# Attention: divisions of a pair in one step of 256 columns, and weight tiles scaled by ScalarE, signed by GpSimd and joined in two VectorE steps

## The chip, the core and the metric

One core of a Trainium2 chip runs the whole program. The metric is the device time of one execution in microseconds (us). TensorE (PE), VectorE (DVE), ScalarE (ACT) and GpSimd (POOL) each run their own instructions in order; SyncE (SP) and GpSimd's queue issue DMAs. An instruction that waits for another engine or for a DMA waits on a semaphore, and all that is queued behind it on its engine waits with it.

## The reference

All arrays are float32, except that the four large weight matrices (w_ch1, w_ch2, w_in, w_out) reach the kernel as float64: NumPy's division by a float64 root makes them so.

```
scores = q @ k.T / sqrt(64) + bias        # q, k, v: 4 batches, 8 heads, 576 rows, 64
scores = where(0 <= rel < 128, scores, -1e9)
attn   = exp(scores - max(scores))
attn   = attn / (sum(attn) + 1e-9)
x      = (attn @ v), heads joined         # 4 x 576 x 512
xn     = (x - mean) / sqrt(var + 1e-6) * g_ln
x      = x + relu(xn @ w_ch1) @ w_ch2     # 512 -> 2048 -> 512
h      = relu(x @ w_in)                   # 512 -> 1024
gate   = sigmoid(conv of 3 taps over the rows of h)
out    = (h * gate) @ w_out               # 1024 -> 512
```

## The kernel before

**Attention (L700 to L944).** Its 72 tiles (a tile is 128 query rows of two heads) go through a software pipeline that is written out by hand: 18 iterations, k = 0 to 17, of four tiles each, in two pairs a and b. In each, TensorE makes the scores of a pair in PSUM (`ps`, L737); VectorE joins two blocks (L748) and takes minima (L752); ScalarE makes the exponentials with their sums (L762, four of 128 columns in a pair); `shares` (L767) divides: VectorE adds 1e-9 and takes the reciprocal, and of a pair's four blocks of 128 columns the two of the even heads are multiplied by VectorE, those of the odd heads by GpSimd (L774). TensorE turns the shares (L784), ScalarE copies them (`pc`, L789), GpSimd masks them twice (`select_p`, L796), TensorE multiplies by v (L812), ScalarE writes the result into `x` (`outputs`, L825). TensorE also turns the q and k of the next tiles (`turn_qk`, L711), and ScalarE copies them (`qt`, `kt`, L838). One iteration's code holds work of three: scores of iteration k, shares of k-1, values of k-2 and outputs of k-3.

**Weights in the attention.** The chip has no float64, so a weight is made from its two 32-bit words, in four steps on a tile of 128 x 512: the high word is taken as a float and multiplied by 2^-112 (`rescale`, L350 on; on GpSimd L358, on ScalarE L356); VectorE shifts left by 3 and masks (part 0, L373), sets the sign bit from the high word (part 1, L378) and the lowest 3 bits from the low word (part 2, L383). Then ScalarE writes a rounded copy (high, L412), VectorE the rest (low, L415). Twelve tiles are converted in this way during the attention. `weights_step` does one step of a tile at a time, and `extras` (L841) calls it twice in an iteration: between `shares` of pair b of the iteration before and `values`, that is ahead of the new exponentials, and once at the end of the iteration. `FINE_START` and `FINE_AT` say in which of these half steps: the load, three half steps later the rescale, and then one step in each half step. So a rescale always falls ahead of the exponentials in the code, and a load at an iteration's end, on SP's queue, behind the loads of q, k and v for later tiles. These write into buffers that `turn_qk` must have read. The raw words of three tiles have room at a time.

**After the attention.** From L944 on the work is put in order by the class `Plan` (L36): each operation is given with its engine, a duration, the memory that it reads and writes, and for some an earliest time (`late`); `schedule` then picks, again and again, the operation that can start first, among those ready on an engine the one that is due first, with DMAs no further than 3 us ahead of a modelled bandwidth. The instructions are issued in that order. Twenty more weight tiles are converted here (`convert_next`, `convert` at L1047) from five raw slots: signs on GpSimd (`signs`, L364: the high word times 0.0, which leaves its sign), rescale on ScalarE, one VectorE step that shifts and joins the sign (L1064), part 2, the high copy, and the low part by a two-operand step of GpSimd (L1236). The matrix products of this stage are L1035.

Of the kernel before, what the change touches and what calls it, by code (L numbers as in the profile page):

```python
# [14 lines left out]
ALU = mybir.AluOpType  # L15
# [20 lines left out]
class Plan:  # L36
# [58 lines left out]
    def schedule(self, pe, goal, succ, cost, rate, landing, wait):  # L95
# [14 lines left out]
        free = {}  # L110
        lock = 0.0
        dma = 0.0
# [98 lines left out]
def tile_kernel(  # L211
# [183 lines left out]
    FINE = (("rescale",), (0,), (1,), (2,), ("high",), ("low",))  # L395

    def weights_step(stages, start=True, only=None):
# [3 lines left out]
        for j in range(max((len(do) for _, do in now), default=0)):  # L401
            for ld, do in now:
                if j >= len(do):
                    continue
                kind, i, raw = ld["kind"], ld["i"], ld["raw"]
                if do[j] == "rescale":
                    t = ld["t"] = fav(FA_CV0 + cvn[0] % 3 * 512, 512).bitcast(I32)
                    cvn[0] += 1
                    rescale(t, raw, G)
                elif do[j] == "high":  # L410
                    w = wtile(kind, i)
                    S.activation(w[:, 0, :], ld["t"].bitcast(F32), AF.Copy)  # L412
                elif do[j] == "low":
                    w = wtile(kind, i)
                    V.tensor_tensor(  # L415
                        out=w[:, 1, :], in0=ld["t"].bitcast(F32), in1=w[:, 0, :].bitcast(F32),
                        op=ALU.subtract,
                    )
                    flight.remove(ld)
                else:  # L420
                    to_f32(ld["t"], raw, (do[j],), ld["mid"])
        if todo and start:
# [9 lines left out]
            else:  # L432
# [3 lines left out]
                "kind": kind, "i": i, "pool": pool, "t": None, "mid": None, "only": only,  # L436
# [100 lines left out]
    with ExitStack() as actx:  # L537
# [229 lines left out]
        def shares(n: int):  # L767
# [5 lines left out]
            for i in range(4):  # L773
                (G if i % 2 else V).tensor_scalar(  # L774
                    out=pp[:, i, :], in0=pp[:, i, :], scalar1=sm[:, 1, i : i + 1], scalar2=1.0,
                    op0=ALU.mult, op1=ALU.mult,
                )
# [63 lines left out]
        def extras(n: int, m: int):  # L841
            for args in fine_at.get(n // 2 + m, ()):
                weights_step(FINE, *args)
# [201 lines left out]
    BF0 = 2000  # L1045

    def convert(kind: str, i: int, raw, cv, mid=None, eng="V"):  # L1047

        late_at = BF0 if raw is None else 0
        src = {"w1": w_ch1, "win": w_in, "w2": w_ch2, "wout": w_out}[kind]  # L1050
        if kind in ("w1", "win"):
            dma(
                raw.rearrange("p (c f) -> p c f", f=2 * P),
                src[:, 2 * i * P : 2 * (i + 1) * P].rearrange("(c p) f -> p c f", p=P), 524288,
            )
        else:
            dma(raw, src[i * P : (i + 1) * P, :], 524288)
# [165 lines left out]
    def convert_next():  # L1223
# [6 lines left out]
        convert(kind, f, raw, cv, MIDS[n % len(MIDS)])  # L1230
# [688 lines left out]
```

## Time and profile before

| | |
|---|---|
| time, median of 3 runs (lowest to highest) | 737.68 us (733.99 to 738.47) |
| the profiled execution, its span | 736.93 us, 735.2 us |
| TensorE busy | 712.5 us (97%) |
| VectorE busy | 526.2 us (72%) |
| ScalarE busy | 402.6 us (55%) |
| GpSimd busy | 238.3 us (32%) |
| the last chain of work | TensorE 71%, VectorE 12%, DMA 5%, GpSimd 5%, ScalarE 3% |

The shares of the whole span are means over stages: the attention ends near 147 us, and behind it come matrix products alone, with TensorE busy nearly throughout. So a stage's limit is read from the stage: from a table of the busy time in a stretch, and from the rows of an engine's timeline, where the number in brackets is the idle time just before an instruction and who ended it. Neighbouring instructions of an engine overlap at their ends, so what an instruction takes from its engine is read from two starts rather than from its duration.

### The profile page before, as it was taken

The numbers are of one execution on the slowest core, as the hardware profiler recorded it, in microseconds if no ns is written. First come the engines' busy times: TensorE is split into PE (matmuls) and PEld (weight loads), VectorE is DVE, ScalarE is ACT, GpSimd is POOL, SyncE is SP. The second block draws the span as 40 slices with busy tenths as digits, with TensorE's granted clock in tenths as the row PEclk, the third lists the DMA queues.
The fourth block names the chain that finished last, engine by engine and source line by source line (L and its number), as shares of the span: only waits on it lengthen the run. The fifth ranks groups of instructions, "written<-read, shape, count | busy, mean of one in ns | idle before, by whom it ended". The sixth has DMA issues, their size and how long they took to land.

```text
span 735.2 us, 13451 instructions
## 1 busy us (share of the span) xinstructions
PE 712.5 (97%) x4704; PEld 664.9 (90%) x4704; DVE 526.2 (72%) x1053; ACT 402.6 (55%) x1050; POOL 238.3 (32%) x408
## 2 busy tenths in 40 slices
PE   7999998899989999999999999999999999999998
PEld 6777876799989999999999999999999898998887
DVE  6799999567979726556679654568468998787731
ACT  4888877645424423333346333344377787776741
POOL 1778789759741202321220233242421000000000
PEclk9999999999999999999999999999999999999999
DMA  6777766238519926986860599996933000000011
GB/s 152 177 179 175 198 155 187 71 104 273 189 35 339 292 70 177 275 265 223 258 211 12 174 267 305 285 276 200 272 93 87 15 30 15 30 15 29 29 47 55
DMA packets 122303, 114.63 MB, mean 156 GB/s; under 512 B 63552, under 2 KB 87292, under 8 KB 122236
## 3 DMA queue, kind: packets, MB, share of 16 engines
q1 hardware_dynamic: 101020, 76.81, 34.6%
q0 software_dynamic: 20160, 36.71, 18.4%
q8 instruction: 37, 0.61, 0.3%
q10 hardware_dynamic: 1056, 0.26, 0.2%
q14 instruction: 30, 0.25, 0.1%
HBM read 80.70 MB, written 33.05 MB: 155 GB/s over the span
## 4 chain that ended last, share of the span: by engine, by line
PE 71%; DVE 12%; DMA 5%; POOL 5%; ACT 3%; issue 3%; SPq 0%; POOLq 0%; ACTq 0%; DVEq 0%
PE bank L1035 65%; DMA wind<-r 2%; PE ps L737 2%; DVE ps L748 2%; DVE pp L774 2%; DMA fa<-in_moe_w_in 1%; DVE mn L752 1%; POOL pt L796 1%; PE po L812 1%; DVE fa L383 1%; PE ptp L784 1%; POOL pp L774 1%; DVE fa L378 1%; ACT fa L996 1%; DMA xnb<-in_moe_w_ch 1%
## 5 line engine op out<-in xcount | busy, mean ns | idle before, releaser
L1035 PE MATMUL bank<-hhr,r 128*128 128x384 f32 x1152 | 214.0, 338 | 0.5 <-DVE fa L1003 0.5
L1035 PE MATMUL bank<-r,r 128*128 128x288 f32 (+1 forms) x1248 | 203.9, 314 | 1.3 <-ACT fa L996 1.1
L1035 PEld LDWEIGHTS bank<-hhr,r 128*128 128x128 f32 x1152 | 199.6, 188 | 2.5 <-DVE fa L1003 1.6
L1035 PEld LDWEIGHTS bank<-r,r 128*128 128x128 f32 x1248 | 193.9, 188 | 4.7 <-ACT fa L996 1.9
L1332 POOL DMA_DIRECT2D r<-w1d x96 | 51.9, 543 | 180.9 <-PE bank L1035 171.8
L996 ACT ACTIVATE fa<-bank 128x288 f32<-128x288 f32 (+1 forms) x112 | 49.8, 445 | 73.0 <-PE bank L1035 71.7
L1035 PE MATMUL bank<-r 128*128 128x512 f32 (+2 forms) x360 | 81.7, 372 | 0.1
L1035 PEld LDWEIGHTS bank<-r 128*128 128x128 f32 x360 | 63.6, 188 | 9.8 <-ACT r L1782 0.5
L996 ACT ACTIVATE r<-fa 128x256 fp32r<-128x256 f32 (+2 forms) x94 | 48.0, 521 | 39.0 <-DMA wind<-r 13.5
L996 ACT ACTIVATE hhr<-bank 128x384 fp32r<-128x384 f32 x46 | 22.5, 490 | 75.5 <-PE bank L1035 75.4
L1003 DVE TENSOR_TENSOR fa<-bank,fa 128x288 f32<-128x288 f32 (+1 forms) x88 | 43.6, 500 | 27.3 <-ACT fa L996 14.6
L762 ACT ACTIVATE pp<-ps,mn 128x128 f32<-128x128 f32 x144 | 51.4, 384 | 12.2 <-DVE mn L752 8.8
L774 POOL TENSOR_SCALAR pp<-pp,sm 128x128 f32<-128x128 f32 x72 | 43.6, 616 | 32.5 <-DVE sm L771 29.9
L1011 DVE SCALAR_TENSOR_TENSOR fa<-fa,cw 128x576 f32<-128x576 f32 x64 | 51.2, 813 | 1.5 <-ACT fa L996 0.7
L1003 DVE TENSOR_TENSOR r<-fa,r 128x256 fp32r<-128x256 f32 (+1 forms) x74 | 37.7, 521 | 19.3 <-ACT r L996 13.1
L1011 DVE SCALAR_TENSOR_TENSOR hhr<-bank,hhr 128x384 fp32r<-128x384 f32 x46 | 25.4, 552 | 35.2 <-ACT hhr L996 35.0
L796 POOL TENSOR_SCALAR_AFFINE_SELECT pt<-pc 128x512 f32<-128x512 f32 x72 | 46.7, 679 | 1.7 <-ACT pc L789 1.4
L737 PE MATMUL ps<-kt,qt 64*128 64x256 f32 x288 | 44.1, 400 | 2.6 <-ACT pp L762 1.7
L812 PE MATMUL po<-pt,rawv 128*64 128x128 f32 x544 | 37.9, 280 | 7.4 <-POOL pt L796 4.9
L1035 PE MATMUL bank<-r,hhr 128*128 128x512 f32 (+1 forms) x192 | 44.6, 381 | 0.0
L812 PEld LDWEIGHTS po<-pt,rawv 128*64 128x64 f32 x544 | 28.9, 136 | 16.0 <-POOL pt L796 12.6
L996 ACT ACTIVATE fa<-fa 128x576 f32<-128x576 f32 (+1 forms) x64 | 39.1, 620 | 2.7 <-DVE fa L1003 1.6
(146 smaller groups left out, 1138.0 us busy)
## 6 DMA issues: line engine op xcount, KB each, us to landing
r<-w1d POOLq DMA_DIRECT2D x96, 256.0 KB, 4.8
fa<-in_moe_w_ch SPq DMA_DIRECT2D x24, 512.0 KB, 4.8
w1d<-r SPq DMA_DIRECT2D x40, 256.0 KB, 3.5
wind<-r SPq DMA_DIRECT2D x28, 256.0 KB, 4.5
r<-wind POOLq DMA_DIRECT2D x28, 256.0 KB, 4.8
out<-h SPq DMA_DIRECT2D x17, 256.0 KB, 2.0
rawq<-in_q SPq DMA_DIRECT2D x32, 128.0 KB, 3.6
rawv<-in_v SPq DMA_DIRECT2D x32, 128.0 KB, 2.8
```

What stands on the lines that cost most here:

```text
L378: V.scalar_tensor_tensor(out=mid, in0=raw[..., 1], scalar=-0x80000000, in1=mid, op0=ALU.bitwise_and, op1=ALU.bitwise_or,)
L737: T.matmul(ps[:, h, u, :].rearrange("p (o j) -> p o j", o=2), lhs, rhs, start=i == 0, stop=i == 1,)
L748: V.copy_predicated(out=sc, mask=own4, data=ps[:, :, :, P:W])
L762: S.activation(pp[:, u, h, :], sc[:, h, u], AF.Exp, bias=mn[:, h, u : u + 1], scale=-1.0, accum_out=sm[:, 0, i : i + 1],)
L774: (G if i % 2 else V).tensor_scalar(out=pp[:, i, :], in0=pp[:, i, :], scalar1=sm[:, 1, i : i + 1], scalar2=1.0, op0=ALU.mult, op1=ALU.mult,)
L796: G.affine_select(out=parts[:, i], in_=pc, compare_op=ALU.is_ge, fill=0.0, base=base, pattern=[[0, 4], [sign, P]], channel_multiplier=-sign,)
L812: T.matmul(po[h * D : (h + 1) * D, u, :], rvs[bl, pr][:, t - 1 + i, h, :], pt[:, i, 2 * u + h, :], start=i == i0, stop=i == 1,)
L996: lambda: S.activation(now(out), now(src), func, **kw),
L1003: "V", tt_ns(cols(out)), lambda: V.tensor_tensor(out=out, in0=a, in1=b, op=op),
L1011: lambda: V.scalar_tensor_tensor(out=now(out), in0=now(a), scalar=sc, in1=now(b), op0=op0, op1=op1),
L1035: T.matmul(out, lhs, now(rhs), start=start and n == 0, stop=stop and n == len(items) - 1, skip_group_check=True,)
L1332: plan.add("G", 560, lambda: nc.gpsimd.dma_start(dst, src), [src], [dst], nbytes=262144)
```

## The change

1. `shares`: VectorE's two steps of 128 columns, each times a factor per row, become one step of 256 columns (the two even heads' blocks), times the two factors spread over the columns. GpSimd's two stay.
2. Weight tiles in the attention: the rescale goes from GpSimd to ScalarE ("scale"), for ten of twelve tiles into a scratch area `xnb` instead of the tile's own place; GpSimd writes the sign one half step later ("sign"); one VectorE step shifts and joins the sign ("first", in the place of parts 0 and 1), and part 2 follows ("last"). Two tiles (`BY_STEPS`) have the scale on ScalarE and parts 0, 1 and 2 as before.
3. The planner: SP and the modelled bandwidth are free from -1e4 ns on, and the first five conversions' loads may start at -1e4, -1e4, -2e3, -2e3 and -2e3 ns.

```diff
@@ -107,9 +107,9 @@
         ready = {}
         est = [op["late"] for op in ops]
         end = [0.0] * n
-        free = {}
+        free = {"SP": -1e4}
         lock = 0.0
-        dma = 0.0
+        dma = -1e4
         pe_at = 0
 
         def put(i):
@@ -392,7 +392,9 @@
 
 
 
-    FINE = (("rescale",), (0,), (1,), (2,), ("high",), ("low",))
+    FINE = (("scale",), ("sign",), ("first",), ("last",), ("high",), ("low",))
+    FINE_S = (("scale",), (0,), (1,), (2,), ("high",), ("low",))
+    BY_STEPS = (17, 19)
 
     def weights_step(stages, start=True, only=None):
 
@@ -403,10 +405,24 @@
                 if j >= len(do):
                     continue
                 kind, i, raw = ld["kind"], ld["i"], ld["raw"]
-                if do[j] == "rescale":
+                if do[j] == "scale":
                     t = ld["t"] = fav(FA_CV0 + cvn[0] % 3 * 512, 512).bitcast(I32)
                     cvn[0] += 1
-                    rescale(t, raw, G)
+                    if ld["steps"]:
+                        rescale(t, raw, S)
+                    else:
+                        o = 2048 + cvn[0] % 2 * 512
+                        ld["mid"] = xnb[:, o : o + 512]
+                        rescale(ld["mid"], raw, S)
+                elif do[j] == "sign":
+                    signs(ld["t"], raw)
+                elif do[j] == "first":
+                    V.scalar_tensor_tensor(
+                        out=ld["mid"], in0=ld["mid"], scalar=3, in1=ld["t"],
+                        op0=ALU.logical_shift_left, op1=ALU.bitwise_or,
+                    )
+                elif do[j] == "last":
+                    to_f32(ld["t"], raw, (2,), ld["mid"])
                 elif do[j] == "high":
                     w = wtile(kind, i)
                     S.activation(w[:, 0, :], ld["t"].bitcast(F32), AF.Copy)
@@ -433,7 +449,7 @@
                 src = (w_ch2 if kind == "w2" else w_out)[i * P : (i + 1) * P, :]
                 nc.sync.dma_start(raw, src)
             flight.append({
-                "kind": kind, "i": i, "pool": pool, "t": None, "mid": None, "only": only,
+                "kind": kind, "i": i, "pool": pool, "t": None, "mid": None, "only": only, "steps": stages is FINE_S,
                 "raw": raw.rearrange("p (n two) -> p n two", two=2), "stages": list(stages),
             })
 
@@ -770,8 +786,11 @@
             V.tensor_scalar(out=sm[:, 1], in0=sm[:, 0], scalar1=1e-9, scalar2=None, op0=ALU.add)
             V.reciprocal(out=sm[:, 1], in_=sm[:, 1])
             pp = live["pp", n].rearrange("p u h j -> p (u h) j")
-            for i in range(4):
-                (G if i % 2 else V).tensor_scalar(
+            even = live["pp", n][:, :, 0, :]
+            r = sm[:, 1].rearrange("p (u h) -> p u h", h=2)[:, :, 0:1].broadcast_to([P, 2, P])
+            V.tensor_tensor(out=even, in0=even, in1=r, op=ALU.mult)
+            for i in (1, 3):
+                G.tensor_scalar(
                     out=pp[:, i, :], in0=pp[:, i, :], scalar1=sm[:, 1, i : i + 1], scalar2=1.0,
                     op0=ALU.mult, op1=ALU.mult,
                 )
@@ -840,7 +859,7 @@
 
         def extras(n: int, m: int):
             for args in fine_at.get(n // 2 + m, ()):
-                weights_step(FINE, *args)
+                weights_step(FINE_S if FINE_START[args[1]] in BY_STEPS else FINE, *args)
             for u in (n + 2 * m, n + 2 * m + 1):
                 if u in SMALL_AT:
                     small_inputs(SMALL_AT.index(u))
@@ -1042,19 +1061,16 @@
         reads = [a for it in items for a in it]
         plan.add("T", ns * len(items), go, reads, [out])
 
-    BF0 = 2000
-
-    def convert(kind: str, i: int, raw, cv, mid=None, eng="V"):
-
-        late_at = BF0 if raw is None else 0
+    def convert(kind: str, i: int, raw, cv, mid=None, late_at=0):
+
         src = {"w1": w_ch1, "win": w_in, "w2": w_ch2, "wout": w_out}[kind]
         if kind in ("w1", "win"):
             dma(
                 raw.rearrange("p (c f) -> p c f", f=2 * P),
-                src[:, 2 * i * P : 2 * (i + 1) * P].rearrange("(c p) f -> p c f", p=P), 524288,
+                src[:, 2 * i * P : 2 * (i + 1) * P].rearrange("(c p) f -> p c f", p=P), 524288, late_at,
             )
         else:
-            dma(raw, src[i * P : (i + 1) * P, :], 524288)
+            dma(raw, src[i * P : (i + 1) * P, :], 524288, late_at)
         rp = raw.rearrange("p (n two) -> p n two", two=2)
         if mid is not None:
             plan.add("G", 702, lambda: signs(cv, rp), [raw], [cv])
@@ -1227,7 +1243,7 @@
         conv_n[0] += 1
         raw = RAWS[n % len(RAWS)]
         cv = fav(FA_CV0 + (cvn[0] + n) % NCV * 512, 512).bitcast(I32)
-        convert(kind, f, raw, cv, MIDS[n % len(MIDS)])
+        convert(kind, f, raw, cv, MIDS[n % len(MIDS)], (-1e4, -1e4, -2e3, -2e3, -2e3)[n] if n < 5 else 0)
         w = wtile(kind, f)
         cvf = cv.bitcast(F32)
         act(w[:, 0, :], cvf)
```

Lines after: L774 becomes L793, L796 L815, L789 L808, L825 L844, L412 L428, L762 L778, L996 L1015; the merged step is L791, "first" L420.

On ScalarE, iteration 6, before: from the copy of turned shares to the exponentials (`pp<-ps`); `x<-po` is `outputs`, `r_62<-fa` the high copy. A wait named DMAHW is for a DMA.

```order
L789 ACTIVATE pc_861<-ptp_825 128x512 [waits PE_49,Activation_49]
L825 ACTIVATE x<-po_768 128x512
L412 ACTIVATE r_62<-fa 128x512 [waits DVE_49]
L762 ACTIVATE pp_899,sm_900<-ps_839,mn_868 128x128 [waits DVE_49,PE_49]
L762 ACTIVATE pp_899,sm_900<-ps_839,mn_868 128x128 x3
L762 ACTIVATE pp_905,sm_906<-ps_852,mn_871 128x128 [waits DVE_49,PE_49,Pool_49]
L762 ACTIVATE pp_905,sm_906<-ps_852,mn_871 128x128
```

The same place of the change:

```order
L808 ACTIVATE pc_850<-ptp_814 128x512 [waits PE_49,Activation_49]
L844 ACTIVATE x<-po_758 128x512
L428 ACTIVATE r_62<-fa 128x512 [waits DVE_49]
L356 ACTIVATE xnb<-fa 128x512 [waits DMAHW7_49]
L778 ACTIVATE pp_887,sm_888<-ps_828,mn_857 128x128 [waits DVE_49,PE_49]
L778 ACTIVATE pp_887,sm_888<-ps_828,mn_857 128x128 x3
L778 ACTIVATE pp_893,sm_894<-ps_841,mn_860 128x128 [waits DVE_49,PE_49,Pool_49]
```

Between the high copy and the exponentials stands the scale step, with a wait for the load of its tile.

On GpSimd, iterations 5 to 6, before: `pt<-pc` masks, `pp<-pp` divides, `fa<-fa` is the rescale.

```order
L796 AFFINE_SELECT pt_863<-pc_861 128x512 [waits Activation_49]
L796 AFFINE_SELECT pt_863<-pc_861 128x512
L774 TENSOR_SCALAR pp_791<-pp_791,sm_792 128x128 [waits DVE_49]
L774 TENSOR_SCALAR pp_791<-pp_791,sm_792 128x128
L358 TENSOR_SCALAR fa<-fa 128x512 [waits DMAHW7_49]
L774 TENSOR_SCALAR pp_899<-pp_899,sm_900 128x128 [waits DVE_49,PE_49,Activation_49]
L774 TENSOR_SCALAR pp_899<-pp_899,sm_900 128x128 [waits Activation_49]
L796 AFFINE_SELECT pt_922<-pc_920 128x512 [waits Activation_49]
L796 AFFINE_SELECT pt_922<-pc_920 128x512
```

The same place of the change:

```order
L815 AFFINE_SELECT pt_852<-pc_850 128x512 [waits Activation_49]
L815 AFFINE_SELECT pt_852<-pc_850 128x512
L793 TENSOR_SCALAR pp_781<-pp_781,sm_782 128x128 [waits DVE_49]
L793 TENSOR_SCALAR pp_781<-pp_781,sm_782 128x128
L793 TENSOR_SCALAR pp_887<-pp_887,sm_888 128x128 [waits DVE_49,PE_49,Activation_49]
L793 TENSOR_SCALAR pp_887<-pp_887,sm_888 128x128 [waits Activation_49]
L815 AFFINE_SELECT pt_909<-pc_907 128x512 [waits Activation_49]
L815 AFFINE_SELECT pt_909<-pc_907 128x512
L364 TENSOR_SCALAR fa<-fa 128x512 [waits DMAHW7_49]
L815 AFFINE_SELECT pt_974<-pc_972 128x512 [waits Activation_49]
L815 AFFINE_SELECT pt_974<-pc_972 128x512
```

The rescale between two pairs of divisions is gone, and the sign step with its wait for the load stands between two pairs of masks of the next code.

On ScalarE, the first conversions behind the attention, before: `L356` rescales, `hhr<-bank` copies a product of TensorE, `r<-fa` are high copies.

```order
L825 ACTIVATE x<-po_2336 128x512 [waits PE_49]
L356 ACTIVATE bank_2374<-xnb 128x512 [waits DMAHW0_49,Activation_49]
L996 ACTIVATE hhr<-bank_2372 128x384 [waits DVE_49,PE_49]
L356 ACTIVATE xnb<-fa 128x512 [waits DMAHW3_49,DMAHW1_49]
L996 ACTIVATE r_62<-fa 128x512 [waits DVE_49]
L356 ACTIVATE xnb<-xnb 128x512 [waits DMAHW2_49]
L996 ACTIVATE r_2364<-fa 128x512 [waits DMAHW5_49,DMAHW4_49,DMAHW6_49,DMAHW3_49,DMAHW7_49,DVE_49,Pool_49]
```

The same place of the change:

```order
L844 ACTIVATE x<-po_2300 128x512 [waits PE_49]
L356 ACTIVATE bank_2338<-xnb 128x512 [waits DMAHW0_49,Activation_49]
L356 ACTIVATE xnb<-xnb 128x512 [waits DMAHW1_49]
L356 ACTIVATE xnb<-fa 128x512 [waits DMAHW2_49]
L1015 ACTIVATE r_62<-fa 128x512 [waits DVE_49]
L1015 ACTIVATE hhr<-bank_2336 128x384 [waits PE_49]
L356 ACTIVATE xnb<-fa 128x512 [waits DMAHW3_49,DVE_49]
L1015 ACTIVATE r_62<-fa 128x512
```

Three rescales stand in a row, where one did, and the copy that waits for TensorE comes behind them and a high copy.

## Rows read from the trace of the kernel before

**Rows 1.** Stretches table, attention: each engine's busy time, granted clock, DMA share, GB/s.
```profile
22.00:132.60 110.60, 103.35 (x1097) 82.88 (x1097) 104.37 (x241) 92.17 (x369) 91.12 (x145) 1.00 0.71 172
```

**Rows 2.** Timeline of ScalarE: start, duration, line, tiles, idle before; first exponentials.
```profile
29.85 0.37 ACT L762 ACTIVATE pp<-ps,mn 128x128 f32<-128x128 f32 x1 [0.79 <-DVE mn L752]
...
50.38 0.37 ACT L762 ACTIVATE pp<-ps,mn 128x128 f32<-128x128 f32 x1 [0.57 <-DVE mn L752]
...
56.95 0.37 ACT L762 ACTIVATE pp<-ps,mn 128x128 f32<-128x128 f32 x1
...
78.33 0.37 ACT L762 ACTIVATE pp<-ps,mn 128x128 f32<-128x128 f32 x1 [0.28 <-DVE mn L752]
...
93.27 0.37 ACT L762 ACTIVATE pp<-ps,mn 128x128 f32<-128x128 f32 x1 [0.99 <-DVE mn L752]
...
116.20 0.37 ACT L762 ACTIVATE pp<-ps,mn 128x128 f32<-128x128 f32 x1 [1.10 <-DVE mn L752]
...
132.65 0.43 ACT L762 ACTIVATE pp<-ps,mn 128x128 f32<-128x128 f32 x1
```

**Rows 3.** Timeline of TensorE: first scores of iterations 3 and 4.
```profile
26.93 0.70 PE L737 MATMUL ps<-kt,qt 64*128 64x256 f32 x4
...
33.35 0.70 PE L737 MATMUL ps<-kt,qt 64*128 64x256 f32 x4
```

**Rows 4.** Timeline of TensorE and stretches table, 200 to 210 us.
```profile
204.39 1.34 PE L1035 MATMUL bank<-xna,r 128*128 128x384 f32 x4 [2.49 <-POOL r L1236]
...
200.00:210.00 10.00, 7.51 (x34) 7.19 (x34) 7.13 (x13) 3.71 (x7) 9.51 (x11) 0.83 0.12 44
```

**Rows 5.** Timeline of VectorE, part of iteration 5.
```profile
45.39 0.60 DVE L774 TENSOR_SCALAR pp<-pp,sm 128x128 f32<-128x128 f32 x2
45.91 0.70 DVE L378 SCALAR_TENSOR_TENSOR fa<-fa 128x512 int32<-128x512 int32 x1
46.53 0.26 DVE L770 TENSOR_SCALAR sm<-sm 128x4 f32<-128x4 f32 x1
```

**Rows 6.** Groups by line and form: count, busy time, mean ns; L373 in 20:260.
```profile
L774 DVE TENSOR_SCALAR pp<-pp,sm 128x128 f32<-128x128 f32 x72 | 25.4, 394 | 1.3
...
L1003 DVE TENSOR_TENSOR xna<-fa,xna 128x256 fp32r<-128x256 f32 x16 | 6.5, 417 | 0.0
...
L1064 DVE SCALAR_TENSOR_TENSOR xnb<-xnb,fa 128x512 int32<-128x512 int32 x13 | 16.2, 1247 | 0.3
...
L1064 DVE SCALAR_TENSOR_TENSOR bank<-bank,fa 128x512 int32<-128x512 int32 x7 | 4.8, 691 | 5.9 <-ACT bank L356 3.2 <-POOL fa L364 2.7
...
L356 ACT ACTIVATE xnb<-fa 128x512 f32<-128x512 f32 x8 | 5.3, 663 | 0.0
...
L373 DVE TENSOR_SCALAR fa<-fa 128x512 int32<-128x512 int32 x12 | 6.4, 531 | 0.0
```

**Rows 7.** Timeline of GpSimd: rescales that waited for a load.
```profile
53.77 0.68 POOL L358 TENSOR_SCALAR fa<-fa 128x512 f32<-128x512 f32 x1 [0.92 <-DMA fa<-in_moe_w_ch]
...
68.09 0.70 POOL L358 TENSOR_SCALAR fa<-fa 128x512 f32<-128x512 f32 x1 [1.18 <-DMA fa<-in_moe_w_ch]
...
81.27 0.67 POOL L358 TENSOR_SCALAR fa<-fa 128x512 f32<-128x512 f32 x1 [0.51 <-DMA fa<-in_moe_w_ch]
```

**Rows 8.** Timeline of SP's queue: weight loads and one input load.
```profile
26.28 0.50 SPq L434 DMA_DIRECT2D fa<-in_moe_w_ch  x1
...
38.92 0.60 SPq L550 DMA_DIRECT2D rawq<-in_q  x1
...
48.88 0.43 SPq L434 DMA_DIRECT2D fa<-in_moe_w_ch  x1
...
113.07 0.44 SPq L434 DMA_DIRECT2D fa<-in_moe_w_ch  x1
```

**Rows 9.** DMA issues of the page: count, KB each, us to landing.
```profile
fa<-in_moe_w_ch SPq DMA_DIRECT2D x24, 512.0 KB, 4.8
```

**Rows 10.** Timeline of ScalarE, start of the next stage.
```profile
150.99 0.49 ACT L996 ACTIVATE hhr<-bank 128x384 fp32r<-128x384 f32 x1 [3.25 <-PE bank L1035]
```

## The prediction

> **What bounds the kernel now.** I read the table by stretches first. In the attention, from 22 to 132.6 us, VectorE is busy 104.37 of 110.60 us (94%), TensorE 103.35, ScalarE 92.17 (83%), GpSimd 91.12 (82%) [rows 1]: four engines are near their limit, so the order of their steps matters as much as their sums. Seventeen iterations of four tiles each follow one another; the first exponentials of iteration k on ScalarE, which I call E_k, are the clock that I use: E_3 29.85, E_6 50.38, E_7 56.95, E_10 78.33, E_12 93.27, E_15 116.20, E_17 132.65 [rows 2]. Where E_k waits, it waits for VectorE's minima (0.79 us at E_3, 0.57 at E_6, 1.10 at E_15). From E_6 to E_17 an iteration takes 82.27/11 = 7.48 us. TensorE bounds how far this can shrink: between 26.93 and 33.35 its scores come round without a gap of the engine, 6.42 us [rows 3].
>
> After the attention TensorE sets the end. There is one gap of its own, 2.49 us before 204.39, for GpSimd's low part of a weight tile; in that stretch the granted clock is 0.83 against 1.00 before, a mean of the 2.4 and the 1.2 GHz level [rows 4]. At 0.83, a third of 10 us ran at half speed: 3.4 us, of which 1.7 are lost. So the gap costs some 4.2 us in all.
>
> **The change, part by part.**
>
> *The merged division.* It removes 36 pairs of 128-column VectorE steps; a pair is 0.52 us by its starts (45.39 to 45.91) [rows 5], and adds 36 steps of 256 columns. No such step with a broadcast factor is in the trace; the bounds are two steps of 0.394 (no gain) and the 256-column two-operand step L1003, 0.417 [rows 6], of which some 0.07 is overlap with the next one, so 0.35. I take 0.35, a gain of 0.17 each, 6 us for all 36.
>
> The Trainium skill, "VectorE: DVE Perf Modes", the perf-mode tier table, speaks against the merge: a float32 step with a scalar per partition runs up to double rate from SBUF, one with two tensors at the single rate only. By its figures, as an estimate, 256 columns at the single rate stream 0.13 us longer than two times 128 at the double one, which leaves some 0.06 of the 0.19 that an instruction saves, 2 us in all instead of 6. The row of 0.417 agrees with the single rate; that the pairs of before run at the double one no run here shows.
>
> *The weight tiles.* For ten of twelve tiles L373 (0.531 us alone, about 0.47 by starts) goes away, because shift and sign become one two-operand step in the place of L378 [rows 6]. Its price: L378, alone 0.70, takes 0.62 by starts (45.91 to 46.53) [rows 5], and the step of this very form in the later stage costs 0.691 where one operand is in PSUM and 1.247 in the mean where both are in SBUF [rows 6]. I take L378's, whose two inputs are in SBUF as well, since GpSimd has only one-operand steps beside it here as there. VectorE then gives back 10 x 0.47 = 4.7 us, with the divisions 10.8 us, about 0.8 in a full iteration. GpSimd has a sign step for its rescale, of the same size, later in the iteration: I cost that at nothing, since its 82% leave 1.3 us of an iteration free; if that cover were gone it is 0.65 us in each of ten iterations.
>
> ScalarE gets 12 scale steps, 0.663 us alone [rows 6]; neighbours overlap at their ends, so I take 0.52 of its time. It is busy 83% of 7.48 = 6.2 us in an iteration, with the scale 6.7, by starts some tenths less: about TensorE's floor of 6.42. An iteration without waits so falls to 6.5, and the most that the attention can gain is VectorE's 10.8 us less what that floor keeps: of 0.8 to 0.9 in a full iteration some 0.7 arrive, 8.75 us in all.
>
> *The new wait, which decides.* A scale step must wait until its tile's load has landed. Before, GpSimd's rescale waited for it, in the middle of the iteration; E_k did not. Now it stands on ScalarE directly ahead of E_k, with eight exponentials, copies of turned tiles and through them TensorE's next scores queued behind it. The loads come late: GpSimd waited for them at 53.77 (iteration 6), 68.09 (8) and 81.27 (10) [rows 7], against E_6 of 50.38 and E_10 of 78.33. With a scale of 0.52 behind the same landing, iteration by iteration:
> - E_3 not before 26.28 (issue of the second load, [rows 8]) + 4.8 (landing, [rows 9]) + 0.55 = 31.7: +1.85 on 29.85.
> - E_6 not before 53.77 + 0.52 = 54.3: +3.9 on 50.38.
> - E_8 and E_10: E_10 not before 81.27 + 0.52 = 81.8: +3.5 on 78.33.
> - E_15 not before 113.07 [rows 8] + 4.8 + 0.55 = 118.4: +2.2 on 116.20.
>
> Between them the faster VectorE pays back: from E_10 to E_12 14.94 becomes 2 x 6.5 (-1.8), and E_15 to E_17 16.45 becomes 2 x 7.4 (-1.6); -0.1 from E_6 to E_7. How the waits add up depends on SP. Each late load stands in SP's queue behind a row of input loads (14 of about 0.6 us ahead of 48.88), whose buffers TensorE's transposes release; the row ahead of 48.88 began at 38.92 [rows 8]. If that schedule moves with TensorE, the waits add: 1.85 + 3.9 - 0.1 + 3.5 - 1.8 + 2.2 - 1.6 = +8.0. If SP's issues stay where they are, only the last one counts: 118.4 + 14.85 = 133.25 against 132.65, +0.6. I take +7, since the waits that begin SP's rows are for TensorE. After E_17 the last two iterations have fewer VectorE steps: -0.5.
>
> *The start of the next stage.* The planner's earlier times let ScalarE issue three scales in a row instead of one, where before the second stood behind a copy that waited for TensorE until 150.99 (3.25 us) [rows 10]. The first conversions come about 3 us earlier. GpSimd's queue changes too: the two-operand low parts stand behind more sign steps. TensorE's order is the same in the whole program, so all there is to win is the gap with its clock, 4.2 us; to lose, about 1 (two sign steps more in front of the low part, as long as GpSimd's rescales of 0.66 to 0.70 [rows 7]). I take -3, as the gap of 2.49 is less than the 3 us and some of the clock goes with it.
>
> Sum: +7 - 0.5 - 3 = +3.5. The profiled execution took 736.93 us (span 735.2), so 740.4; it lies 0.75 below the median of 737.68, within their spread of 733.99 to 738.47. I say 740.5.
>
> **Rivals.**
> (A) *Faster: the waits don't hold ScalarE*, since a faster VectorE lets TensorE release SP's buffers earlier, and the loads land before each scale is due. For it: VectorE sets E_k wherever it waits. Against: GpSimd, which met the loads later in the iteration, still waited. Then -8.75 in the attention, -4.2 after it: 736.93 - 12.95 = 724.0. Chance 0.20, with the cases in which only one or two loads bind (about 730).
> (B) *Slower: VectorE's two-operand steps and GpSimd hold each other up*, so that the shortening goes. Price: 10 x (1.247 - 0.691) = 5.6 us on "first", and the paybacks of 3.5 between waits vanish; with the +8.0 of above and nothing won in the next stage: 736.93 + 8.0 + 3.5 = 748.4 (the 5.6 are the larger sum, of which the lost 3.5 are what shows). It decides once an iteration without waits takes 7.3 us instead of 6.5. Against it is L378's 0.70. Chance 0.24, with those in which the next stage starts late. The Trainium skill, "SBUF — State Buffer", the section on its two separate sides, has a rule by which it would go so: VectorE and GpSimd share a pair of ports that one instruction holds alone when VectorE's has two inputs in SBUF and GpSimd's reads SBUF. By that rule the trace agrees in the later stage (1.247 against 0.691) and does not in the attention (0.70).
> (C) *The planner's part does nothing*: the gap before 204.39 stays although the first conversions start earlier, because GpSimd's low parts (busy 9.51 of 10 us there [rows 4]) and not the starts are the limit. Then +6.5: 743.4. It lies within the forecast's range. Chance 0.20, my forecast itself 0.36.
>
> **Numbers.** What a measurement of this kernel can tell from no change is about 1%: 730.3 to 745.1. Forecast and (C) lie inside that, 0.56; (A) below, 0.20; (B) above, 0.24. The range reaches from 728 (the near part of A, two of four waits binding) to 748 (B); the likeliest case alone would be 733 to 746.
>
> **What would show it.** Right, if ScalarE's rows after show idle time "for a DMA" ahead of the scale step in iterations 3, 6, 8, 10 and 15, of some 2 to 4 us each, and E_17 falls near 139; if VectorE's busy time falls by about 10 us with its share below 90% in the attention; if the merged step is near 0.42 and "first" near 0.70; and if the gap before 204 is gone with a granted clock of 1.00. Wrong, if scale steps start without a wait (then A), if "first" runs over 1 us (B), or if TensorE idles elsewhere after the attention (C).

## The result and the profile after

The changed kernel takes 741.93 us, median of 13 runs (739.33 to 745.77), the kernel before 736.07 us in 13 runs beside them (733.92 to 738.97): a ratio of 1.0073, 95% interval 1.0057 to 1.0089. It is slower by 0.7%, 5.9 us, within 1% as forecast (740.5 us). The profiled execution of the changed kernel took 739.33 us (span 737.6), 2.4 us more than that of before; it is the fastest of the 13, and why the median lies 2.6 us above it is told last.

The stretches of [rows 1] and [rows 4] in the changed kernel (columns: span, busy time of TensorE, its weight loads, VectorE, ScalarE and GpSimd with counts, granted clock, DMA share, GB/s):

```profile
22.00:132.60 110.60, 95.88 (x1030) 77.61 (x1028) 87.52 (x191) 92.48 (x364) 88.16 (x136) 1.00 0.71 171
...
200.00:210.00 10.00, 10.00 (x63) 9.92 (x62) 7.91 (x14) 3.94 (x7) 7.96 (x7) 1.00 0.24 83
```

VectorE's busy time fell from 104.37 to 87.52 us in the same 110.6 us, but less was done in them: TensorE is down from 103.35 to 95.88 with 1030 instead of 1097 instructions. From 200 to 210 us the gap is gone and the granted clock is 1.00 instead of 0.83; nor does TensorE have a gap from 210 to 300 us, where the same work now falls.

ScalarE's timeline shows where the attention lost its time. L356 is the scale step, L778 the first exponentials that come right behind it:

```profile
23.49 0.69 ACT L356 ACTIVATE xnb<-fa 128x512 f32<-128x512 f32 x1 [1.70 <-DMA fa<-in_moe_w_ch]
...
30.64 0.69 ACT L356 ACTIVATE xnb<-fa 128x512 f32<-128x512 f32 x1 [1.12 <-DMA fa<-in_moe_w_ch]
...
31.23 0.35 ACT L778 ACTIVATE pp<-ps,mn 128x128 f32<-128x128 f32 x1
...
38.59 0.68 ACT L356 ACTIVATE xnb<-fa 128x512 f32<-128x512 f32 x1 [1.39 <-DMA fa<-in_moe_w_ch]
...
53.91 0.70 ACT L356 ACTIVATE xnb<-fa 128x512 f32<-128x512 f32 x1 [2.31 <-DMA fa<-in_moe_w_ch]
...
54.52 0.34 ACT L778 ACTIVATE pp<-ps,mn 128x128 f32<-128x128 f32 x1
...
68.99 0.70 ACT L356 ACTIVATE xnb<-fa 128x512 f32<-128x512 f32 x1 [1.93 <-DMA fa<-in_moe_w_ch]
...
84.30 0.69 ACT L356 ACTIVATE fa<-fa 128x512 f32<-128x512 f32 x1 [2.28 <-DMA fa<-in_moe_w_ch]
...
84.89 0.34 ACT L778 ACTIVATE pp<-ps,mn 128x128 f32<-128x128 f32 x1
...
123.53 0.68 ACT L356 ACTIVATE xnb<-fa 128x512 f32<-128x512 f32 x1 [2.94 <-DMA fa<-in_moe_w_ch]
...
124.12 0.34 ACT L778 ACTIVATE pp<-ps,mn 128x128 f32<-128x128 f32 x1
```

Seven of the twelve scale steps waited for their load, for 1.12 to 2.94 us and 13.67 us in all. The exponentials of iterations 3, 6, 10 and 15 start at 31.23, 54.52, 84.89 and 124.12, where they started at 29.85, 50.38, 78.33 and 116.20 [rows 2]. The chain of work that ended last, between 49 and 62 us, runs through one of these loads: SP's input loads, the weight load for 4.17 us, the scale, the exponentials.

```profile
49.06 0.49 SPq L579
...
49.73 4.17 DMA fa<-in_moe_w_ch
...
53.91 0.02 ACT xnb L356
...
54.52 0.17 ACT pp L778
```

What ScalarE waited for from 20 to 140 us (in total us, times, longest), after:

```profile
ACT xnb L356 <- DMA fa<-in_moe_w_ch: 11.4, 6, 2.9
...
ACT fa L356 <- DMA fa<-in_moe_w_ch: 2.3, 1, 2.3
...
ACT pp L778 <- DVE mn L768: 1.4, 4, 0.8
```

and from 20 to 135 us before:

```profile
ACT pp L762 <- DVE mn L752: 8.8, 11, 1.3
```

The 8.8 us of waits for VectorE's minima became 1.4 (3.2 with one of 1.75 before 16.81 us, ahead of this stretch), and 13.7 us of waits for loads came in their place.

The steps that the change touches, as groups (count, busy us, mean ns, idle before), and GpSimd's divisions before:

```profile
L793 POOL TENSOR_SCALAR pp<-pp,sm 128x128 f32<-128x128 f32 x72 | 49.7, 701 | 38.1 <-DVE sm L787 35.9 <-PE ptr L727 0.9 <-ACT kt L857 0.5
...
L791 DVE TENSOR_TENSOR pp<-pp,sm 128x256 f32<-128x256 f32 x36 | 15.8, 438 | 1.2
...
L420 DVE SCALAR_TENSOR_TENSOR xnb<-xnb,fa 128x512 int32<-128x512 int32 x10 | 7.3, 727 | 0.0
```

```profile
L774 POOL TENSOR_SCALAR pp<-pp,sm 128x128 f32<-128x128 f32 x72 | 43.6, 616 | 32.5 <-DVE sm L771 29.9 <-PE ptp L784 1.6 <-ACT kt L838 0.5
```

The merged step took 0.438 us and "first" 0.727. GpSimd's divisions, which the change leaves as they were, went from 0.616 to 0.701 us.

### The profile page after: what moved, and what is told of

Same layout as the page of the kernel before. It is cut to its first block, busy times and chain, and to the rows that moved or that the text cites. A ratio compares the mean times of both kernels' runs of the same rounds, so it can differ in the third digit from the quotient of the medians.

```text
span 737.6 us, 13434 instructions
## 1 busy us (share of the span) xinstructions
PE 709.1 (96%) x4704; PEld 663.0 (90%) x4704; DVE 511.7 (69%) x1007; ACT 409.1 (55%) x1062; POOL 241.8 (33%) x406
## 4 chain that ended last, share of the span: by engine, by line
PE 75%; DMA 7%; ACT 5%; DVE 4%; SPq 3%; POOL 3%; issue 2%; ACTq 0%; POOLq 0%; DVEq 0%
PE bank L1054 68%; DMA wind<-r 3%; ACT pp L778 2%; SPq L579 2%; PE ps L753 2%; DMA fa<-in_moe_w_ch 2%; DMA fa<-in_moe_w_in 2%; PE po L831 1%; POOL pt L815 1%; PE ptp L803 1%; POOL pp L793 1%; PE bank L1110 1%; ACT fa L1015 1%; SPq L569 1%; PE busy L627 1%
## 5 line engine op out<-in xcount | busy, mean ns | idle before, releaser
L1015 ACT ACTIVATE fa<-bank 128x288 f32<-128x288 f32 (+1 forms) x112 | 49.8, 445 | 72.4 <-PE bank L1054 70.9
L1015 ACT ACTIVATE r<-fa 128x256 fp32r<-128x256 f32 (+2 forms) x94 | 47.8, 522 | 37.5 <-DVE fa L383 12.8
L793 POOL TENSOR_SCALAR pp<-pp,sm 128x128 f32<-128x128 f32 x72 | 49.7, 701 | 38.1 <-DVE sm L787 35.9
L1015 ACT ACTIVATE hhr<-bank 128x384 fp32r<-128x384 f32 x46 | 22.6, 491 | 68.1 <-PE bank L1054 67.9
L778 ACT ACTIVATE pp<-ps,mn 128x128 f32<-128x128 f32 x144 | 51.3, 385 | 3.2 <-DVE mn L768 3.2
L815 POOL TENSOR_SCALAR_AFFINE_SELECT pt<-pc 128x512 f32<-128x512 f32 x72 | 44.3, 640 | 1.7 <-ACT pc L808 1.3
L1015 ACT ACTIVATE fa<-fa 128x576 f32<-128x576 f32 (+1 forms) x64 | 39.0, 620 | 2.5 <-DVE fa L1022 1.4
```

The costliest lines, as they stand in the source:

```text
L778: S.activation(pp[:, u, h, :], sc[:, h, u], AF.Exp, bias=mn[:, h, u : u + 1], scale=-1.0, accum_out=sm[:, 0, i : i + 1],)
L793: G.tensor_scalar(out=pp[:, i, :], in0=pp[:, i, :], scalar1=sm[:, 1, i : i + 1], scalar2=1.0, op0=ALU.mult, op1=ALU.mult,)
L815: G.affine_select(out=parts[:, i], in_=pc, compare_op=ALU.is_ge, fill=0.0, base=base, pattern=[[0, 4], [sign, P]], channel_multiplier=-sign,)
L1015: lambda: S.activation(now(out), now(src), func, **kw),
```

## The experiments

Theory L is the prediction's: the scale step's wait for its load, ahead of the exponentials, is what costs. Its rivals: C, VectorE's two-operand steps and GpSimd hold each other up; S, ScalarE's twelve more steps cost by themselves. Behind these stood a second question: whether VectorE's work set the pace at all (D), or a ring of several engines' steps (R).

**The scale half an iteration later.** The scale goes to the iteration's end, beside the sign:

```diff
-    FINE_AT = (0, 3, 4, 5, 6, 7, 8)
+    FINE_AT = (0, 4, 5, 6, 7, 8)
-    FINE = (("scale",), ("sign",), ("first",), ("last",), ("high",), ("low",))
-    FINE_S = (("scale",), (0,), (1,), (2,), ("high",), ("low",))
+    FINE = (("scale", "sign"), ("first",), ("last",), ("high",), ("low",))
+    FINE_S = (("scale",), (0, 1), (2,), ("high",), ("low",))
```

> The changed kernel with one edit: the scale step of a weight tile stands half an iteration later in the code, at the iteration's end beside the sign, so that ScalarE has issued the exponentials before it waits for the load; all work is kept. Theory L (the scale's wait for its load, ahead of the exponentials, is what costs): ScalarE's idle time for loads ahead of scale steps falls from 13.7 us (seven waits) to under 4, the joins of the last iteration come about 7 to 10 us earlier than at 136.5, the time is 731 to 735. Rival C (VectorE's two-operand steps and GpSimd hold each other up) and rival S (twelve more steps on ScalarE are what costs): nothing of theirs is changed, the time stays at 740 to 743.

734.54 us (12 runs), 0.9971 of the kernel before (0.9950 to 0.9991): 7.4 us less than the changed kernel, as L has it, and no wait of ScalarE for a load is left in the attention. All of the change's work is still there, so neither C nor S can be the main cost. In the profiled execution the last iteration's first join came at 132.72 us, 3.8 us earlier than in the changed kernel and not 7 to 10; from 120 to 124 us its granted clock was 0.57.

**The merged division alone** (the kernel before with part 1 of the change):

> The kernel before with the merged division alone. Theory L: no wait is added, VectorE has some 3 to 6 us less to do in the attention and sets its pace there, so the time falls by 2 to 5 us, 731 to 734. Rival C: the two-operand step on pp holds GpSimd's divisions up (they take 0.70 us each in the changed kernel against 0.62), GpSimd's masks come later, 736 or more.

736.02 us, 1.0000 (0.9983 to 1.0016). My forecast of 2 to 5 us was a miss. VectorE's busy time in the whole execution fell from 526.2 to 518.7 us, and GpSimd's rose from 238.3 to 245.1, with its divisions at 0.676 us instead of 0.616: most of what the one saved, the other got.

**The planner's earlier times alone:**

> The kernel before with the planner's earlier times alone. My step for the next stage: TensorE's gap of 2.49 us before 204.39 and the lower clock around it go, -3 to -4 us, 732 to 733. Rival: the gap goes only because the shifted attention has given the loads more time; then the gap stays here and the time is 736.

734.61 us, 0.9975 (0.9954 to 0.9996): the gap before 204.39 is gone, with a clock of 1.00 from 200 to 210 us (below), so this part does what the prediction says, but for 1.7 us instead of 3 (by the interval, 0.3 to 3.4).

```profile
200.00:210.00 10.00, 10.00 (x61) 9.96 (x61) 7.78 (x15) 3.85 (x7) 6.48 (x9) 1.00 0.07 26
```

**The weight tiles' new steps alone** (part 2, with the old divisions and planner times):

> The kernel before with the weight tiles' new steps alone (scale on ScalarE, sign, first, last), old divisions, old planner times. Theory L: the load waits of the changed kernel (some 13 us on ScalarE) without the divisions' gain and without the planner's: 743 to 747. Rival C puts the loss on the divisions and expects about 736; rival S, with 12 x 0.52 us on ScalarE against 4.7 us less on VectorE, 736 to 738.

742.79 us (6 runs), 1.0090 (1.0068 to 1.0113): +6.4 us. So the loss sits in this part. The three parts by themselves give +6.4, -0.3 and -1.7, together +4.4, against the whole's 5.9; the intervals, each more than 1 us to either side, leave room for that difference.

**The loads earlier.** The other way to take the wait away: at an iteration's end SP issues the weight load ahead of the loads of q, k and v. Only SP's order changes.

```diff
-        def extras(n: int, m: int):
+        def weights(n: int, m: int):
             for args in fine_at.get(n // 2 + m, ()):
                 weights_step(FINE_S if FINE_START[args[1]] in BY_STEPS else FINE, *args)
+
+        def extras(n: int, m: int):
+            if m == 0 or n >= NS:
+                weights(n, m)
...
+            weights(n, 1)
             for u in range(n + 4, n + 8):
```

> The changed kernel with one edit: at an iteration's end SP issues the weight load ahead of that iteration's loads of q, k and v instead of behind them; the order of the compute engines stays. Theory L (ScalarE's scale waits for a late load): the loads of iterations 6, 10 and 15 are issued up to 8 us earlier, the waits ahead of scale steps fall from 13.7 us to under 5, and the time to about that of the late scale, 734 to 737. Rival: the input loads come later instead and TensorE waits for them, 739 to 743.

733.30 us, 0.9965 (0.9948 to 0.9982), 8.6 us less than the changed kernel and a little less than expected. The fourth load, issued at 49.73 there, goes out at 37.12, and of the seven waits one is left:

```profile
37.12 0.37 SPq L450 DMA_DIRECT2D fa<-in_moe_w_ch  x1
...
22.93 0.69 ACT L356 ACTIVATE xnb<-fa 128x512 f32<-128x512 f32 x1 [1.12 <-DMA fa<-in_moe_w_ch]
```

Two different cures give nearly the same time. The wait for the load, ahead of the exponentials, is the cause.

**What VectorE's work is worth.** Three runs ask it. The late scale with the old divisions:

> The late scale (734.5 us) with the old divisions, two VectorE steps of 128 columns. Rival C (the merged step slows GpSimd's divisions from 0.62 to 0.70 us, which takes back what VectorE gains): 732 to 734.5, GpSimd's divisions back at 0.62. Theory D (VectorE's work sets the pace once the wait is gone): 6 us more on VectorE, 738 to 741. Theory R (neither: a ring of ScalarE, TensorE and VectorE steps sets an iteration): 734 to 735.

733.94 us, 0.9970 (0.9955 to 0.9986), no slower than with the merged step (734.54). The early loads with the old divisions:

> The changed kernel with early loads (733.3 us) and the old divisions. Theory C (what the merged step saves on VectorE, GpSimd's slower divisions take back): 732.5 to 734, GpSimd's divisions at 0.57 to 0.60 us instead of 0.70. Theory D (VectorE sets the pace): 736 to 738.

732.55 us, 0.9958 (0.9945 to 0.9972), against 733.30 with the merged step. GpSimd's divisions with the merged step, and then without it:

```profile
L793 POOL TENSOR_SCALAR pp<-pp,sm 128x128 f32<-128x128 f32 x72 | 49.5, 697 | 31.6 <-DVE sm L787 28.2 <-PE ptr L727 1.3 <-ACT pc L808 0.9
```

```profile
L790 POOL TENSOR_SCALAR pp<-pp,sm 128x128 f32<-128x128 f32 x72 | 41.1, 581 | 37.4 <-DVE sm L787 31.8 <-PE ptp L800 2.7 <-ACT pc L805 1.4
```

0.697 against 0.581 us. Three pairs of kernels (before, late, early) differ by the merged step alone; it changes the time by -0.3, +0.6 and +0.75 us. As shares of the kernel before, run beside each, the pairs differ by 0.00, 0.01 and 0.07%, so no gain and no loss can be told. And the kernel before with less work for VectorE, the shift and mask of twelve tiles left out:

> The kernel before with VectorE's shift-and-mask step (L373) of the twelve weight tiles in the attention left out, nothing put in its place (the weights are then not those of the reference). Theory D (VectorE sets the attention's pace, 94% busy): 12 x 0.47 = 5.6 us less on VectorE, time -4 to -5.6, 731 to 732.5. Theory R (a ring of ScalarE's exponentials and copies, TensorE's scores, VectorE's joins, at some 7.2 us an iteration): -0 to -2, 734.5 to 736.5.

733.21 us, 0.9967 (0.9949 to 0.9986): 2.7 us (1.0 to 3.8) for 5.6 us of VectorE's work, between what D and R expected. In the attention itself its last iteration's first join came at 128.80 instead of 130.60 (the kernel before, then this one):

```profile
130.60 0.68 DVE L748 COPY_PREDICATED ps<-own,ps 128x512 f32<-128x512 int32 x1
```

```profile
128.80 0.68 DVE L748 COPY_PREDICATED ps<-own,ps 128x512 f32<-128x512 int32 x1
```

That is 1.8 us, although the granted clock from 14 to 16 us was 0.50 in this execution and 1.00 in the kernel before. So a third to a half of what VectorE saves arrives, even when no other engine gets more to do.

**The scale back on GpSimd,** in its old place, with the sign half an iteration later as in the change:

> The changed kernel with the scale steps back on GpSimd at their old place, so that ScalarE has neither the steps nor the waits; GpSimd has scale and sign, 12 more steps of 0.66 us. Theory L: 13.7 us of ScalarE's waits go; GpSimd, 82 to 86% busy, takes 0.66 us more in each of twelve iterations and meets the loads 2 to 3 us later in an iteration: 734 to 738. Rival S and C: 740 or more.

736.54 us, 1.0012 (0.9992 to 1.0033): 5.4 us less than the changed kernel, with none of ScalarE's waits for a load left, but 3.2 more than with early loads. GpSimd is then busy 83.33 of 94 us (78.75 with early loads):

```profile
22.00:116.00 94.00, 89.33 (x936) 70.79 (x934) 82.50 (x173) 78.13 (x316) 83.33 (x131) 1.00 0.74 177
```

**The early loads in the kernel before,** as a control:

> The kernel before with the early loads alone (SP issues an iteration's weight load ahead of its loads of q, k and v). Theory L: in the kernel before nothing on the path waited for these loads (GpSimd's 2.6 us were covered), so nothing comes of it: 735 to 736.5. Rival: early loads are worth the same 8.6 us in any kernel, because they shift the traffic; then 728 to 731.

734.18 us, 0.9988 (0.9974 to 1.0002): less than expected, but no difference that can be told from none. Of the 8.6 us that the early loads gave the changed kernel, at most 2 would so be a gain of any kernel; the rest is its own wait. With the planner's times too:

> The kernel before with the early loads and the planner's earlier times: the changed kernel with early loads (733.3 us) without the merged division and without the weight tiles' new steps. If the new steps and the division are worth nothing even when no load holds ScalarE, this is 732.5 to 734.5; if VectorE's 15 us less are worth their share, it is 736 or more.

732.40 us, 0.9967 (0.9950 to 0.9984). This kernel is the changed one with early loads, without the merged step and without the new steps of the weight tiles, and it is no slower (732.4 against 733.3). From 22 to 116 us, this kernel and then the changed one with early loads:

```profile
22.00:116.00 94.00, 89.04 (x948) 71.52 (x944) 89.13 (x208) 78.83 (x322) 76.88 (x125) 1.00 0.75 181
```

```profile
22.00:116.00 94.00, 89.02 (x952) 71.80 (x948) 80.13 (x177) 85.85 (x338) 78.75 (x123) 1.00 0.75 179
```

VectorE's busy time is 9.0 us less in the second, ScalarE's 7.0 us more, and TensorE's is the same, 89.0 of 94 us. The first join of iterations 2 and 14, in the same order:

```profile
21.21 0.70 DVE L748 COPY_PREDICATED ps<-own,ps 128x512 f32<-128x512 int32 x1 [2.18 <-PE ps L737]
...
105.76 0.68 DVE L748 COPY_PREDICATED ps<-own,ps 128x512 f32<-128x512 int32 x1
```

```profile
21.57 0.70 DVE L764 COPY_PREDICATED ps<-own,ps 128x512 f32<-128x512 int32 x1 [2.69 <-PE ps L753]
...
105.01 0.69 DVE L764 COPY_PREDICATED ps<-own,ps 128x512 f32<-128x512 int32 x1 [0.17 <-PE ps L753]
```

Twelve iterations take 84.55 and 83.44 us, 7.05 and 6.95 each. The nine microseconds of VectorE buy 1.1. By the last iteration nothing is left of that: its first join comes at 129.37 and 129.89 us. In the second kernel TensorE had to wait for GpSimd's masks before 116.96, and its granted clock was lower behind it:

```profile
116.96 1.33 PE L831 MATMUL po<-pt,rawv 128*64 128x128 f32 x10 [2.09 <-POOL pt L815]
...
116.00:120.00 4.00, 3.04 (x20) 2.71 (x21) 3.93 (x7) 0.70 (x4) 4.00 (x6) 0.61 0.48 107
```

**Both cures together:**

> The changed kernel with both cures, the late scale and the early loads. Theory L: each alone removed nearly all of the wait, so both together give no more than the better: 732 to 734.5. If a part of the wait had been left in either, 730 to 731.

735.21 us, 0.9994 (0.9977 to 1.0010), a miss: slower than with early loads alone. TensorE's waits for ScalarE's copies of turned tiles between 40 and 118 us (total, times, longest), with both cures and then with early loads alone:

```profile
PE ps L753 <- ACT kt L857: 2.6, 7, 0.4
```

```profile
PE ps L753 <- ACT kt L857: 0.3, 1, 0.3
```

The late scale stands on ScalarE ahead of those copies and makes TensorE's scores late by 2.6 us in all. That is a price of the late place itself; the late scale alone paid it too, 3.0 us. From the first join of iteration 2 to that of iteration 14 both cures take 85.28 us, the late scale alone 85.42 and the early loads alone 83.44, which fits the 1.9 us between the two medians. It does not explain everything: the late scale alone, with the same price, took 734.54 us, and the profiled execution with both cures was the faster one (733.92 against 735.53 us). Why both together came out slower than either stays open; the intervals of the two with the late scale overlap.

The best of the changed kernels is the one with early loads and the old divisions, 732.55 us; it beats the changed kernel and, by 0.4%, the kernel before. The kernel before with early loads and the planner's times does as well (732.40).

## Why the prediction was right, point by point

- **The new wait decides.** Right, in place and nearly in size. By E_k, measured against predicted: to iteration 3 +1.38 (+1.85); from 3 to 6 +2.76 (+3.9); 6 to 7 -0.40 (-0.1); 7 to 10 +2.82 (+3.5); 10 to 12 -0.96 (-1.8); 12 to 15 +2.32 (+2.2); 15 to 17 -2.03 (-1.6). The sum is +5.9 where I worked out 8.0 and took 7. The rows of these that are not above:

```profile
60.69 0.36 ACT L778 ACTIVATE pp<-ps,mn 128x128 f32<-128x128 f32 x1
...
98.87 0.37 ACT L778 ACTIVATE pp<-ps,mn 128x128 f32<-128x128 f32 x1 [0.24 <-DVE mn L768]
...
138.54 0.43 ACT L778 ACTIVATE pp<-ps,mn 128x128 f32<-128x128 f32 x1
```

The waits were smaller than forecast (9.3 us in the four steps up, against 11.5), the paybacks as forecast (3.4 against 3.5, in which 14.94 less 2 x 6.5 should have been 1.9 and not 1.8). Two scale steps that I did not name waited too, in iterations 2 (1.70 us) and 4 (1.39), and two of those that I named waited less than the 2 to 4 us that I gave as a sign: 1.12 us in iteration 3 and 1.93 in iteration 8.
- **Whether SP's rows shift with TensorE.** Little at first, fully at the end. The row of input loads that was at 38.92 begins at 39.64 (+0.72, while E_3 had moved by 1.38), the load behind it at 49.73 instead of 48.88; the last is issued at 118.86 instead of 113.07 [rows 8], 5.8 us later, where E_14 had moved by 5.2:

```profile
39.64 0.60 SPq L566 DMA_DIRECT2D rawq<-in_q  x1
...
49.73 0.37 SPq L450 DMA_DIRECT2D fa<-in_moe_w_ch  x1
...
118.86 0.44 SPq L450 DMA_DIRECT2D fa<-in_moe_w_ch  x1
```

- **The gap of the next stage.** It went, as said: from the first join of the last iteration (130.60 before, 136.47 after, +5.87) to the end of the span (+2.4) the changed kernel wins 3.5 us, which is what I put (-0.5 - 3). The single part gave 1.7, and the reason is in the one execution that I sized it by. The changed kernel's join:

```profile
136.47 0.70 DVE L764 COPY_PREDICATED ps<-own,ps 128x512 f32<-128x512 int32 x1
```

Three other kernels without the planner's part have the gap with 0.68 us and a clock of 1.00 from 200 to 210 us, a fourth (the weight tiles' new steps alone) with 1.40; here with the merged division alone and with the early loads alone in the kernel before:

```profile
203.11 0.79 PE L1038 MATMUL bank<-xna,r 128*128 128x384 f32 x3 [0.68 <-POOL r L1239]
...
202.78 0.79 PE L1040 MATMUL bank<-xna,r 128*128 128x384 f32 x3 [0.68 <-POOL r L1241]
```

So 2.49 us with the lower clock were the worst of five executions, and the term of -3 was probably too large for the median; the interval of the single part still reaches it.
- **The merged division.** The step that failed. On VectorE I sized it well: 0.438 us alone, and by starts 0.35 as I took it (46.97 to 47.32 in the changed kernel), so 0.17 each were saved and not the 0.06 of my second estimate. But I let its 6 us count in what an iteration gets back, and by itself it was worth nothing. GpSimd's divisions beside it, which I did not look at, went from 0.616 to 0.701 us in the changed kernel, 72 of them: +6.1 us. By the merged step alone they went from 0.616 to 0.676, from 0.571 to 0.704 (late) and from 0.581 to 0.697 (early). That this is what took the gain back is argued and not shown: no run gave GpSimd the time again. Rival B named the mechanism and set its price on another step ("first", which ran at 0.727, near my 0.70). The mean of 1.247 us that it took the price from has one step of 4.302 us among its thirteen; the median is 0.755 (shortest, median, longest, in ns):

```profile
L1064 DVE SCALAR_TENSOR_TENSOR xnb<-xnb,fa x13: 652/755/4302, 152.6 to 202.3; 128x512 int32<-128x512 int32 x13
```

The Trainium skill, "SBUF — State Buffer", the section on its two separate sides, says that a VectorE step with two inputs in SBUF and a GpSimd step that reads SBUF exclude each other. The trace agrees in direction: GpSimd's divisions took 0.58 us beside one-input divisions and 0.70 beside the two-input one; the two-input "first" showed no such price in its own 0.727.
- **What VectorE's savings pay.** I let some 0.7 to 0.9 us of an iteration arrive and called 8.75 us the most that the attention could win. With no load in the way it won 1.1 in twelve iterations, and nothing by the last. The busy share of 94% said that VectorE had little slack, not that the others had any. TensorE, busy 103.35 of 110.60 us [rows 1], left 7.25 us of that stretch, less than the 8.75 that I called the most, and with early loads it leaves 5.0 of 94. There VectorE waits for TensorE's scores 7.1 us between 40 and 118 us (total, times, longest), and TensorE most of all for GpSimd's masks:

```profile
DVE ps L764 <- PE ps L753: 7.1, 10, 1.4
```

```profile
PE po L831 <- POOL pt L815: 3.6, 5, 2.1
```

ScalarE, with the scale steps, is busy 85.85 of 94 us. The 6.42 us of TensorE, read from one early iteration, were not what twelve iterations could keep. Which step of the ring holds an iteration at about 7 us was not tried and stays open.
- **Rival A** (724 us, loads in time) would have been wrong even with its condition met: with the loads in time the kernel takes 733.3.
- **The range and the chances.** The +3.5 was worked out on one execution, and between the two profiled ones +2.4 was measured; between the medians it is +5.9. So 740.5 came within 1.4 us of 741.93 partly by luck: the waits were put 1 to 2 us too high, and the prediction's start, 736.93 us, lay 0.9 above the later median of the kernel before, while it left out that executions with load waits would run at a lower mean clock (below).

## What to carry to other kernels

When a step is moved to another engine, look first at what it waits for and at what stands behind it in its new queue: a wait that was covered on one engine can be on the path on the next. If the wait is for a load, try to move the load in its queue; that cost nothing here and gave the changed kernel 8.6 us. An engine that is 94% busy is a reason to ask what its neighbours would do with the time: another that is 93% busy leaves little to win. Leaving a piece of the work out, in one run, tells what it is worth at most before anything is rebuilt.

## What the runs showed of the hardware that was not expected

The granted clock fell behind waits of TensorE, and differently from execution to execution. In the profiled execution of the weight tiles' new steps alone, a scale step had waited 3.30 us for its load; TensorE stood for 3.15 us before 74.42 for a copy of ScalarE behind it, and from 76 to 80 us its granted clock was 0.50, the lower of its two levels (1.2 of 2.4 GHz), with TensorE busy all through:

```profile
71.13 0.66 ACT L356 ACTIVATE xnb<-fa 128x512 f32<-128x512 f32 x1 [3.30 <-DMA fa<-in_moe_w_ch]
...
74.42 0.90 PE L800 MATMUL ptp<-ident,pp 128*128 128x128 f32 x3 [3.15 <-ACT pc L805]
...
72.00:76.00 4.00, 1.57 (x6) 1.22 (x8) 2.27 (x6) 4.00 (x22) 2.21 (x3) 0.66 0.42 92
...
76.00:80.00 4.00, 4.00 (x24) 2.98 (x20) 1.39 (x2) 2.19 (x8) 2.45 (x5) 0.50 0.66 150
```

It is not only load waits that do this, and not each time: with early loads the clock fell behind a wait of 2.09 us for GpSimd's masks (above, 116.96), and in the profiled execution of the changed kernel it stayed at 1.00 behind such a wait of 2.08 us, before 123.94.

In the 13 runs of the changed kernel the mean clock of an execution lies between 0.988 and 0.999, on average 0.9934, and the time goes with it: 739.33 us at 0.999, 745.77 at 0.989. In 35 runs of the kernel before it is 0.9967 on average. Of all kernels run, the two with the load waits have the lowest means, this one and the weight tiles' new steps alone (0.9942); with early loads it is 0.9971, and in none of the others below 0.9966. The profiled execution of the changed kernel had none of these spells in its attention. A straight line through its 13 times gives 0.39 us for each 0.001 of the mean clock, through the 35 of the kernel before 0.44. By that, as an estimate, the profiled execution's clock of 0.999 is 2.2 of the 2.6 us by which it lies below its median, and the difference of the two kernels' mean clocks, 0.0033, is 1.3 to 1.5 of the 5.9 us. The rest, some 4.5 us, would be lost at equal clock.
